# Storing most rows of dV of three heads with fifteen of the sixteen DMA engines

## The chip, the core and the metric

The kernel runs on one core of one Trainium2 chip. Its metric is the device time of one execution in microseconds (us). "Span" is the time in the profile from the first to the last instruction of the profiled execution. A ratio of two kernels is the mean time of one kernel's fast runs over that of the other's in the same rounds, so it is not quite the ratio of the medians quoted beside it. "Fast" and "slow" are states of a run: a run over 1.5% above the fastest of its kernel counts as slow and is not compared.

## The reference

Forward and backward of a gated sum of a one-token attention block with a KV cache (A) and a small MLP (B). What matters here is the attention, because of its bytes:

```python
# H = 32 heads, Sk = 4096 cached keys, Dh = 128, bfloat16
scores = einsum("bhqd,bhkd->bhqk", q, k_cache) * Dh ** -0.5
p = softmax(scores)
o = einsum("bhqk,bhkd->bhqd", p, v_cache)
out = g * (o @ wo) + (1 - g) * mlp(x)
# returned: out and the gradients of x, k_cache, v_cache, wq, wo, w1, b1, w2, gate_w
```

K and V are 1 MB per head each and are read once. dK and dV are outer products of the same size and are written once. That is 134 MB (4 x 32 x 1.049) of the 164.9 MB which the core moves.

## The kernel before

Each head has a period: its K and V tiles were loaded three heads ahead on the SP queue, PE transposes and multiplies them, DVE writes the outer products, and POOL (the software DMA queue) stores them.

```python
kv_in = pool(bufs=4)          # Kn and Vn, four buffers each
outs  = pool(bufs=5)          # dK and dV share five buffers

def load_k(h):
    kts[h] = kv_in.tile([P, J, Dh], BF16, name="Kn", ...)   # P=128 partitions x 8 KB
    nc.sync.dma_start(kts[h][:], Kv[h])

def dv_half(h, half):
    st = sts[h]
    if half == 0:
        st["dV"] = outs.tile([P, J, Dh], BF16, name="dV_sb", tag="dVK")
    outer(st["dV"], st["p"], ..., half)
    if half == 1:
        nc.gpsimd.dma_start(dVv[h], st["dV"][:])

# ... (dk_half is alike; loop of heads:)
for h in range(H):
    load_k(h + 3); load_v(h + 3)
    # ...
    period(h)
```

A store of 128 rows of 8 KB has 16 completions in the trace, one for each of the 16 DMA engines; an even share is 8 rows to an engine.

Of the kernel before, what the change touches and what calls it, by code (L numbers as in the profile page):

```python
# [16 lines left out]
def kernel(  # L17
# [24 lines left out]
    nc = tc.nc  # L42
    P = 128
    _, H, Sk, Dh = A_k_cache.shape
    D = A_x.shape[-1]
    F = B_w1.shape[1]
    J = Sk // P
# [20 lines left out]
    dVv = out_3.rearrange("b h (p j) d -> (b h) p j d", p=P)  # L68
# [68 lines left out]
    def load_w2(c):  # L137
# [28 lines left out]
        out=ident_f[:], in_=ident_f[:], compare_op=ALU.not_equal, fill=1.0,  # L166
# [69 lines left out]
    for i in range(3):  # L236
        t = const.tile([P, 2, G, 2, 2], BF16, name=f"qd2_{i}")
# [370 lines left out]
    def outer(dst, col, row, half):  # L608
        n = J // 2
        a, b = half * n, (half + 1) * n  # L610
        nc.vector.tensor_tensor(  # L611
            dst[:, a:b, :].rearrange("p j (a b) -> p j a b", b=2),
            col[:, a:b, :].unsqueeze(2).to_broadcast([P, n, Dh // 2, 2]),
            row.rearrange("p (a b) -> p a b", b=2).unsqueeze(1).to_broadcast([P, n, Dh // 2, 2]),
            ALU.mult)
# [16 lines left out]
# [3 lines that stand above are left out]
            st["dV"] = outs.tile([P, J, Dh], BF16, name="dV_sb", tag="dVK")  # L635
        outer(st["dV"], st["p"], gps[h // G]["qd"][:, 1, (h % G) * Dh:(h % G + 1) * Dh], half)
        if half == 1:
            nc.gpsimd.dma_start(dVv[h], st["dV"][:])  # L638

    def period(h):  # L640
        gp = gps[h // G]
# [11 lines left out]
        def o_part(a, b):  # L653
            for j in range(a, b):
# [31 lines left out]
        nc.vector.scalar_tensor_tensor(pj[:], in0=DP[:, 0:J], scalar=1.0, in1=e[:], op0=ALU.mult, op1=ALU.mult,  # L686
                                       accum_out=part[:])
        dv_half(h, 0)
        nc.tensor.transpose(PT, part[:].to_broadcast([P, P]), ident_f[:])  # L689
        if nxt:  # L690
# [6 lines left out]
        nc.vector.scalar_tensor_tensor(ds[:], in0=DP[:, 0:J].unsqueeze(2).to_broadcast([P, J, 2]), scalar=dd[:], in1=p_bf[:],  # L697
                                       op0=ALU.subtract, op1=ALU.mult)
        dv_half(h, 1)
        nc.vector.tensor_scalar(o_all[:, h:h + 1], O[:, 0:1], rz[:], None, ALU.mult)  # L700
        if nxt:
# [145 lines left out]
```

## Time and profile before

| | before |
|---|---|
| time, median of the first 3 runs | 413.07 us (413.03 to 413.67) |
| span of the profiled run | 411.8 us |
| busiest compute engine | DVE, 74% |
| DMA | nine tenths or more from 10 us to the last slice, 401 GB/s on average |

First the page's slices (each of the 40 is 10.3 us) and its queue table: packets, MB, and the time of the packets as a share of sixteen engines' span.

```profile
DMA  7999999999999999999999999999999999999990
GB/s 293 419 416 400 424 423 415 424 422 423 421 425 422 423 418 421 423 423 420 424 420 423 423 407 420 421 406 386 399 421 419 426 419 422 422 384 372 377 358 14
...
q1 hardware_dynamic: 14404, 82.03, 48.3%
q0 software_dynamic: 12240, 82.03, 48.2%
```

The DMA engines hold the run at about 422 GB/s, and the rate sags in the last five slices. The last slice is the telling one: 14 GB/s over 10 us. The stretches of the tail say more (us from the span's start; busy time and number of instructions of each engine, granted clock, DMA share of sixteen engines, GB/s):

```profile
core 0: us, PE busy (x) PEld busy (x) DVE busy (x) ACT busy (x) POOL busy (x), PEclk, DMA share, GB/s
380.00:395.00 15.00, 4.99 (x122) 3.87 (x119) 13.70 (x39) 1.79 (x6) 5.78 (x8) 0.70 0.96 385
395.00:401.60 6.60, 0.27 (x1) 0.09 (x1) 3.19 (x13) 0.25 (x1) 0.00 (x0) 0.50 0.86 327
401.60:407.20 5.60, 0.00 (x0) 0.00 (x0) 0.00 (x0) 0.00 (x0) 0.00 (x0) 0.50 0.06 26
```

For 5.6 us nothing computes and the DMA share is 0.06, which is one engine of sixteen. It moves 26 GB/s, the pace of one engine. The whole span waits for it.

The trace also records when each of the sixteen engines reports its part of a DMA complete. These times have no engine names. They stand on the clock of the instructions: where PE waits for a load, it starts 0.04 to 0.14 us after the load's last completion. The table shows how far the 16th is behind the 15th. For the loads I used the five of the SP queue's eight semaphores on which every load has sixteen completions.

```
                          gap from the 15th to the 16th completion, us
K/V loads, first ten      0.3 to 2.1
K/V loads, last five      12.0  12.2  13.7  12.2  12.4
last store (dwq_l)        1st 400.6   15th 401.9   16th 407.5   gap 5.6
```

One engine falls behind all others. In the packet records 7,010 of the 8,064 stored rows of 8 KB take 309 ns. One chain of back-to-back packets is slower: from 200.1 us on its rows take 316, 319, 335, 335, 332, 315, 318 and 321 ns. Yet in the drain at the end, when one engine works alone, most 4 KB packets take 159 ns, as they do on other engines at their best. So, if the chain and the drain are the same engine, it is slow only in company. Instruction fetches load the engines too: 46 packets of 16 KB, about 1 us each, 46 us in all. The largest gap among the K/V loads is 13.7 us, so these fetches do not all fall on one engine.

The waits of compute for DMA, from the page's groups (busy us, mean ns, then idle us before the group and who ended most of it):

```profile
L586 PE MATMUL tr<-ident_f,Kn 128*128 128x128 f32 x512 | 82.2, 299 | 6.5 <-DMA Kn<-in_A_k_cache_dram 6.5
L611 DVE TENSOR_TENSOR dK_sb<-ds_bf,qd 128x2048 bf16<-128x2048 bf16 x64 | 77.7, 1215 | 4.4 <-DMA out_dram<-dV_sb 4.4
```

These two are small.

### The profile page before, as it was taken

What the parts mean: (1) busy time and instruction counts of PE and PEld (TensorE: products, weight loads), DVE (VectorE), ACT (ScalarE), POOL (GpSimd) and SP (SyncE); (2) the same over time, 40 slices, a digit from 0 to 9 for tenths busy, and PEclk for the clock granted to TensorE, in tenths of its full rate; (3) what the DMA queues carried; (4) which work ended last, traced back from release to release, by engine and by line L of the source; (5) the groups of instructions that cost most, each with busy time, mean ns of one, the idle gap of its engine ahead of it and who ended that gap; (6) DMA issues with size and microseconds to landing.
All of it is one profiled execution on the core that took longest, in us unless ns stands there. A gap on an engine that the chain in (4) does not pass through costs nothing.

```text
span 411.8 us, 13602 instructions
## 1 busy us (share of the span) xinstructions
PE 296.3 (72%) x5872; PEld 268.2 (65%) x5872; DVE 303.1 (74%) x791; ACT 177.1 (43%) x411; POOL 50.8 (12%) x99
## 2 busy tenths in 40 slices
PE   0688898588887888188887888338887789949300
PEld 0578787587786777178877777338777778848200
DVE  3339666856899999377698898537999997957860
ACT  1355555254545555046542557215554455534000
POOL 0001111000111111011101112001111121113410
PEclk9999999889999999779996999758999999997755
DMA  7999999999999999999999999999999999999990
GB/s 293 419 416 400 424 423 415 424 422 423 421 425 422 423 418 421 423 423 420 424 420 423 423 407 420 421 406 386 399 421 419 426 419 422 422 384 372 377 358 14
DMA packets 26744, 164.93 MB, mean 401 GB/s; under 512 B 2956, under 2 KB 3020, under 8 KB 10428
## 3 DMA queue, kind: packets, MB, share of 16 engines
q1 hardware_dynamic: 14404, 82.03, 48.3%
q0 software_dynamic: 12240, 82.03, 48.2%
q8 instruction: 46, 0.75, 0.7%
q14 instruction: 14, 0.11, 0.1%
q10 hardware_dynamic: 40, 0.01, 0.0%
HBM read 82.03 MB, written 82.03 MB: 398 GB/s over the span
## 4 chain that ended last, share of the span: by engine, by line
DMA 38%; DVE 33%; PE 19%; ACT 4%; issue 3%; POOL 0%; ACTq 0%; SPq 0%; POOLq 0%; DVEq 0%
DMA Kn<-in_A_k_cache_dram 30%; PE tr L586 8%; DVE dK_sb L611 7%; DVE dV_sb L611 7%; DMA out_dram<-dV_sb 6%; DVE junk L382 4%; ACT tT L588 3%; PE sA L655 3%; DVE junk L285 3%; PE sA L595 2%; PE sB L708 2%; DVE junk L534 1%; DVE junk L491 1%; DMA vec_rows<-in_gate_w_dram 1%; DVE dj L695 1%
## 5 line engine op out<-in xcount | busy, mean ns | idle before, releaser
L588 ACT COPY tT<-tr 128x512 f32<-128x512 f32 x256 | 142.2, 587 | 129.7 <-PE tr L586 128.9
L595 PEld LDWEIGHTS <-tT 128*128 128x128 bf16 x2048 | 79.7, 98 | 44.4 <-ACT tT L588 34.5
L586 PE MATMUL tr<-ident_f,Kn 128*128 128x128 f32 x512 | 82.2, 299 | 6.5 <-DMA Kn<-in_A_k_cache_dram 6.5
L611 DVE TENSOR_TENSOR dK_sb<-ds_bf,qd 128x2048 bf16<-128x2048 bf16 x64 | 77.7, 1215 | 4.4 <-DMA out_dram<-dV_sb 4.4
L611 DVE TENSOR_TENSOR dV_sb<-p_bf,qd 128x2048 bf16<-128x2048 bf16 x64 | 77.9, 1218 | 0.2 <-issue 0.2
L586 PE MATMUL tr<-ident_f,Vn 128*128 128x128 f32 x512 | 72.5, 277 | 0.0
L586 PEld LDWEIGHTS tr<-ident_f,Kn 128*128 128x128 f32 x512 | 61.6, 153 | 7.7 <-issue 5.2
L595 PE MATMUL sA<-qd,tT 128*128 128x48 bf16 x1024 | 48.6, 187 | 23.7 <-ACT dq_all L713 12.8
L586 PEld LDWEIGHTS tr<-ident_f,Vn 128*128 128x128 f32 x512 | 55.9, 141 | 0.0
L595 PE MATMUL sB<-qd,tT 128*128 128x48 bf16 x1024 | 46.3, 183 | 0.0
L638 POOL DMA_DIRECT2D out_dram<-dV_sb x32 | 18.2, 569 | 170.2 <-DVE dV_sb L611 58.5
L655 PEld LDWEIGHTS <-Vn 128*128 128x128 bf16 x1024 | 30.6, 96 | 10.4 <-issue 10.4
L655 PE MATMUL sA<-e_bf,Vn 128*128 128x48 bf16 x1024 | 31.2, 184 | 7.6 <-DVE zs L675 6.2
L628 POOL DMA_DIRECT2D out_dram<-dK_sb x31 | 18.3, 591 | 145.3 <-DVE rz L677 97.2
L708 PE MATMUL sB<-ds_bf,Kn 128*128 128x48 bf16 x1024 | 31.5, 184 | 1.4 <-DVE ds_bf L697 1.4
L708 PEld LDWEIGHTS <-Kn 128*128 128x128 bf16 x1024 | 28.9, 97 | 1.6 <-issue 1.6
L659 DVE TENSOR_REDUCE m<-sA 128x1 f32<-128x32 f32 x32 | 6.0, 189 | 32.2 <-PE sA L595 25.6
L285 DVE SCALAR_TENSOR_TENSOR junk<-wo_g,da_bc 128x640 bf16<-128x640 bf16 x32 | 26.2, 820 | 1.7 <-ACT da_bc L226 1.1
L695 DVE TENSOR_SCALAR_CACHE_REDUCE dj<-sB,rz 128x128 f32<-128x128 f32 x32 | 11.1, 345 | 21.3 <-PE sB L689 21.3
L382 DVE SCALAR_TENSOR_TENSOR junk<-wq_g,dq_bc 128x1024 bf16<-128x1024 bf16 (+1 forms) x25 | 25.1, 1005 | 0.2
L275 PE MATMUL qc_ps<-cols_bf,wq_g 128*128 128x1 bf16 x160 | 5.3, 164 | 22.1 <-DMA wq_g<-in_A_wq_dram 22.1
L275 PEld LDWEIGHTS <-wq_g 128*128 128x128 bf16 x160 | 4.8, 100 | 22.6 <-DMA wq_g<-in_A_wq_dram 22.4
(154 smaller groups left out, 280.7 us busy)
## 6 DMA issues: line engine op xcount, KB each, us to landing
Kn<-in_A_k_cache_dram SPq DMA_DIRECT2D x32, 1024.0 KB, 23.9
Vn<-in_A_v_cache_dram SPq DMA_DIRECT2D x32, 1024.0 KB, 29.0
out_dram<-dV_sb POOLq DMA_DIRECT2D x32, 1024.0 KB, 11.8
out_dram<-dK_sb POOLq DMA_DIRECT2D x31, 1024.0 KB, 12.0
wq_g<-in_A_wq_dram SPq DMA_DIRECT2D x4, 1280.0 KB, 30.3
wo_g<-in_A_wo_dram SPq DMA_DIRECT2D x8, 640.0 KB, 7.4
out_dram<-wo_g POOLq DMA_DIRECT2D x8, 640.0 KB, 11.3
out_dram<-dwq_t POOLq DMA_DIRECT2D x5, 896.0 KB, 14.4
```

Of the source, the lines that this page charges most:

```text
L275: nc.tensor.matmul(qc_ps[:, hh:hh + 1], lhsT=wq[:, rc, off + hh * Dh:off + (hh + 1) * Dh], rhs=x_bf[:, rc:rc + 1], start=(rc == 0), stop=( ...
L285: nc.vector.scalar_tensor_tensor(junk[:, 0:D], in0=wos[g][:, i, :], scalar=1.0, in1=da_bc[:], op0=ALU.mult, op1=ALU.mult, accum_out=gp["do ...
L382: nc.vector.scalar_tensor_tensor(junk[:, c0:c1], in0=wqs[w][:, rc, c0:c1], scalar=1.0, in1=dq_bc[:, w * WG * Dh + c0:w * WG * Dh + c1], op ...
L586: nc.tensor.transpose(tp[:, t, :], flat[:, k * P:(k + 1) * P], ident_f[:])
L588: nc.scalar.copy(sb[:].rearrange("p a b -> p (a b)"), tp[:].rearrange("p a b -> p (a b)"))
L595: nc.tensor.matmul(out[:, 2 * k:2 * k + W], lhsT=tb[:, t, par, :], rhs=vec[:, par, :].unsqueeze(1).to_broadcast([P, W // 2, 2]), start=(pa ...
L611: nc.vector.tensor_tensor(dst[:, a:b, :].rearrange("p j (a b) -> p j a b", b=2), col[:, a:b, :].unsqueeze(2).to_broadcast([P, n, Dh // 2, 2]),
L628: nc.gpsimd.dma_start(dKv[h], st["dK"][:])
L638: nc.gpsimd.dma_start(dVv[h], st["dV"][:])
L655: nc.tensor.matmul(O, lhsT=vts[h][:, j, :], rhs=st["e"][:, j:j + 1].to_broadcast([P, W]), start=(j == 0), stop=(j == J - 1))
L695: nc.vector.tensor_scalar(dj[:], PT, rz[:], None, ALU.mult, ALU.add, accum_out=dd[:])
L708: nc.tensor.matmul(DQ, lhsT=kts[h][:, j, :], rhs=ds[:, j, 0:1].to_broadcast([P, W]), start=(j == 0), stop=(j == J - 1))
```

## The change

Intent: take rows away from the slow engine. The Trainium skill, "DMA: Bandwidth & Descriptors", section "Why a DMA increments its semaphore by 16 and not by 1", says that a DMA uses the largest number of engines up to 16 that divides its slowest dimension, and that on the software queue fewer than 16 are taken in a row from a round-robin cursor. By that rule, 5 rows go to positions 0 to 4, 120 rows to the next fifteen (5 to 15 and 0 to 3, 8 rows each), and 3 rows to 4, 5 and 6. Position 4 gets 2 rows instead of 8; positions 0 to 3, 5 and 6 get 9. The trace has no engine numbers, so it can neither confirm nor refute this layout.

```diff
         if half == 1:
-            nc.gpsimd.dma_start(dVv[h], st["dV"][:])
+            if h % 10 == 9:
+                spread(dVv[h], st["dV"])
+            else:
+                nc.gpsimd.dma_start(dVv[h], st["dV"][:])
+
+    def spread(dst, t):
+        src = t[:].rearrange("p j d -> p (j d)")
+        out = dst.rearrange("p j d -> p (j d)")
+        nc.gpsimd.inc_swdge_sem([], [], mode="reset_dge_cursor")
+        for a, b in ((120, 125), (0, 120), (125, 128)):
+            nc.gpsimd.dma_start(out[a:b, :], src[a:b, :], max_dma_last_dim=J * Dh)
```

The last argument splits each 8 KB row into two of 4 KB, which makes the shape of the DMA three-dimensional (120 x 2 x 2048 elements).

## The prediction

> **What bounds the kernel now: the DMA engines, and of the sixteen, one.** The page's slices show DMA at nine tenths from about 10 us to the end at 415 to 425 GB/s, sagging to 358 to 384 in the last five. The queue table: 82.03 MB loaded on q1 and 82.03 MB stored on the software queue q0, 48.3% + 48.2% of sixteen engines' span. No compute engine is above 74%; PE waits only 6.5 us in all for Kn, DVE 4.4 us for a store to free a dV buffer (groups and waits).
>
> In the packet records a full 8 KB row takes 309 ns, about 306 ns from one to the next (26.8 GB/s per engine), on most engines. One chain of packets is slower: 313 to 345 ns per row, about 5%. The sixteen completions of each DMA show the same: for K/V loads the gap from the 15th to the 16th grows from 0.3 us early to 12.4 us late in the run, with the 14th and 15th within about 1 us. Of the last stores (dwq_l, the last dwo, dK halves) the 16th completes 5.6 to 5.7 us after the 15th. The span ends with one engine draining alone for 5.6 us, ten microseconds after compute is done. PE's instruction fetches (46 of 16 KB, about 1 us each) rotate over several engines and don't explain it.
>
> The Trainium skill, "DMA: Bandwidth & Descriptors", section "Latency and other measured facts", says engines 7 and 15 are usually slower in traces where the software queue is used (cause a guess). This trace agrees that one is slower; it doesn't number it.
>
> **What the change does.** Three dV stores of 1 MB (8 rows per engine) become 5 + 120 + 3 rows. By the same page, section "Why a DMA increments its semaphore by 16 and not by 1", a software-queue DMA takes the largest divisor up to 16 of its rows as number of engines, starting from a cursor. So 5 rows on five engines, 120 on the next fifteen (8 each), 3 on the next three: one engine gets 2 rows instead of 8, six get 9. Per run the spared engine loses 18 rows; at about 0.32 us, 5.8 us. Six others gain 3 rows, 0.9 us. Added: six more DMA issues on POOL, 0.53 us each (12% busy, much idle), rows in two 4 KB pieces (159 instead of 154 ns each, nothing), 96 completion writes of 9 ns. Compute order is unchanged.
>
> **How much is critical.** If the spared engine is the slow one, it is busy without a pause to the end, so the span shortens by its relief until another engine ends last: the others end 5.6 us earlier now, and up to 0.9 us later after. Gain: about 4.7 us (range 3.5 to 6). If the slow engine is another one, nothing is won, and 0 to 1 us lost. The cut with a 5-row head and 18 rows of relief against a tail of 5.65 us looks fitted to this engine; I give 0.7 that it hits.
>
> **Predicted: 408.6 us**, 407.2 to 413.6 eight times in ten. Faster by over 2% 0.03, within 2% 0.95, slower 0.02: even a full hit is 1.2%.
>
> **What would show it.** Right: the 15th-to-16th gap of the last stores falls from 5.65 us to under 1.5 us; the late K/V load gap shrinks in steps of about 2 us after heads 9, 19, 29; slices 36 to 40 carry more GB/s; PE's wait for Kn falls. Wrong engine: the gap stays 5.6 us and the 120-row store still completes last on the slow engine.
>
> **What would make it wrong.** The cursor is not where I think, or shapes like this go ceil(rows/16) per engine; the slow engine's pace differs from run to run; two engines slow on another chip.

## The result

| | before | after |
|---|---|---|
| median | 413.33 us (4 runs, 413.03 to 413.67) | 408.69 us (4 runs, 407.98 to 409.01) |
| ratio of fast runs | | 0.9885, 95% interval 0.9867 to 0.9903 |
| span of the profiled run | 411.8 us | 406.6 us |

The time is inside the range and 0.1 us from the figure named. The lines of the page after, which answer to those above:

```profile
GB/s 290 420 416 396 422 422 420 419 423 423 421 425 421 422 420 406 424 425 421 422 420 425 424 421 416 410 424 423 425 420 424 424 421 424 422 402 368 406 394 77
...
q0 software_dynamic: 12912, 82.03, 49.0%
q1 hardware_dynamic: 14404, 82.03, 48.9%
...
L586 PE MATMUL tr<-ident_f,Kn 128*128 128x128 f32 x512 | 84.2, 304 | 9.6 <-DMA Kn<-in_A_k_cache_dram 9.6
L611 DVE TENSOR_TENSOR dK_sb<-ds_bf,qd 128x2048 bf16<-128x2048 bf16 x64 | 77.8, 1216 | 3.9 <-DMA out_dram<-dV_sb 3.6
```

The same stretches of the tail:

```profile
380.00:395.00 15.00, 1.61 (x26) 0.99 (x25) 11.28 (x38) 0.54 (x2) 4.97 (x7) 0.50 1.00 401
395.00:401.60 6.60, 0.00 (x0) 0.00 (x0) 0.00 (x0) 0.00 (x0) 0.00 (x0) 0.50 0.48 191
401.60:407.20 5.60, 0.00 (x0) 0.00 (x0) 0.00 (x0) 0.00 (x0) 0.00 (x0) 0.50 0.00 1
```

The stretch in which one engine worked alone is empty. The completions agree:

```
                          before                          after
K/V loads, last five      12.0 12.2 13.7 12.2 12.4        4.2 4.9 3.8 4.6 4.8
last store, 15th / 16th   401.9 / 407.5                   401.3 / 401.7
```

The gap of the loads drops by about 2 us after each of the first two split stores (2.9 to 1.0 after head 9) and grows again between and after them. When the third is issued, at 355.1 us, only three loads are not yet complete, and their gaps show no drop (4.3, 4.6 and 4.8 us). The slow engine ends 5.8 us sooner, which over 18 rows is 0.32 us per row.

The gain is not only at the tail. Compute runs ahead too: the issue of the last store by POOL, from the timeline of each kernel (start, duration, idle before), is 5.7 us sooner. Before:

```profile
393.20 0.87 POOL L777 DMA_DIRECT2D out_dram<-dwq_l  x1 [0.70 <-DVE ambj L787]
```

After:

```profile
387.51 0.90 POOL L787 DMA_DIRECT2D out_dram<-dwq_l  x1 [0.18 <-DVE ambj L797]
```

### The profile page after: what moved, and what is told of

Same layout as the page of the kernel before. It is cut to its first block, busy times and chain, and to the rows that moved or that the text cites. A ratio compares the mean times of both kernels' runs of the same rounds, so it can differ in the third digit from the quotient of the medians.

```text
span 406.6 us, 13614 instructions
## 1 busy us (share of the span) xinstructions
PE 298.3 (73%) x5872; PEld 269.9 (66%) x5872; DVE 303.8 (75%) x791; ACT 177.2 (44%) x411; POOL 55.7 (14%) x105
## 3 DMA queue, kind: packets, MB, share of 16 engines
q0 software_dynamic: 12912, 82.03, 49.0%
q1 hardware_dynamic: 14404, 82.03, 48.9%
HBM read 82.03 MB, written 82.03 MB: 404 GB/s over the span
## 4 chain that ended last, share of the span: by engine, by line
DMA 36%; DVE 33%; PE 19%; ACT 4%; issue 3%; POOL 0%; ACTq 0%; DVEq 0%; POOLq 0%
DMA Kn<-in_A_k_cache_dram 29%; DVE dK_sb L611 8%; PE tr L586 8%; DVE dV_sb L611 7%; DMA out_dram<-dV_sb 6%; DVE junk L382 4%; ACT tT L588 4%; PE sA L665 3%; DVE junk L285 2%; PE sA L595 2%; PE sB L718 2%; DVE junk L534 1%; DVE junk L491 1%; DMA vec_rows<-in_gate_w_dram 1%; DVE dj L705 1%
## 5 line engine op out<-in xcount | busy, mean ns | idle before, releaser
L586 PE MATMUL tr<-ident_f,Kn 128*128 128x128 f32 x512 | 84.2, 304 | 9.6 <-DMA Kn<-in_A_k_cache_dram 9.6
L586 PEld LDWEIGHTS tr<-ident_f,Kn 128*128 128x128 f32 x512 | 63.0, 155 | 11.3 <-issue 10.5
L641 POOL DMA_DIRECT2D out_dram<-dV_sb x29 | 16.5, 570 | 149.0 <-DVE o_all L710 54.7
L705 DVE TENSOR_SCALAR_CACHE_REDUCE dj<-sB,rz 128x128 f32<-128x128 f32 x32 | 11.1, 346 | 12.8 <-PE sB L699 12.7
L689 ACT ACTIVATE p_bf<-e_bf,rz 128x64 bf16<-128x64 bf16 x32 | 11.1, 348 | 13.6 <-DVE rz L687 10.6
L696 DVE SCALAR_TENSOR_TENSOR pj<-sB,e_bf 128x32 f32<-128x32 f32 x32 | 6.1, 191 | 13.1 <-PE sB L595 12.9
```

What stands on the lines that cost most here:

```text
L586: nc.tensor.transpose(tp[:, t, :], flat[:, k * P:(k + 1) * P], ident_f[:])
L689: nc.scalar.activation(p_bf[:], e[:].unsqueeze(2).to_broadcast([P, J, 2]), ACT.Copy, scale=rz[:])
L705: nc.vector.tensor_scalar(dj[:], PT, rz[:], None, ALU.mult, ALU.add, accum_out=dd[:])
```

## The experiments

Theory: one engine, at position 4 of the software queue's cursor, is slower than the rest and has work queued to the end, so each row taken from it shortens the run by what that row costs it. Rivals: the smaller pieces or the reset help; sparing any engine helps; the gain needs the lag gone altogether; only relief at some moment counts. Twelve kernels ran on two chips (the first four on one, the other eight on the other). All gave correct results.

### Same pieces, no engine spared

```diff
-        for a, b in ((120, 125), (0, 120), (125, 128)):
+        for a, b in ((0, 48), (48, 96), (96, 128)):
```

> The same three heads, also cursor reset and three pieces of 4 KB packets, but 48 + 48 + 32 rows, so that every piece runs on all 16 engines and each engine keeps its 8 rows. Theory (relief of one slow engine): no gain, 413.3 us within 1, last-store gap between the 15th and 16th completion stays 5 to 6 us. Rival (smaller pieces or packets, or the reset, are what helps): about 408.7 us and a gap under 1.5 us.

Measured: 415.15 us, ratio 1.0036 (1.0020 to 1.0051). No gain, so neither pieces nor reset are what helps. It even lost 1.5 us, a little more than the 1 us that the forecast allowed. Its profiled run fell in the slow state (451.24 us, clock 0.573), so its trace can't say why and its gap isn't used. As a control of the early heads (below) the same split on heads 2, 4 and 6 was run:

> The 48 + 48 + 32 split over all 16 engines on heads 2, 4 and 6, as control for the early run. If the 1.5 us that this split cost on heads 9, 19 and 29 is the price of the pieces themselves (packets, completion writes): 414.5 to 415.5 us. If it came from where those stores fell among the semaphores: 413 to 414 us. In either case no gain.

Measured: 413.78 us, ratio 1.0006 (0.9992 to 1.0020), last-store gap 6.2 us. So there the pieces themselves cost nothing that can be measured. The 1.5 us belongs to where the stores stood in the first kernel, or to the chip, as the two kernels ran on different ones. What it was stays open.

### Another engine spared

```diff
-        for a, b in ((120, 125), (0, 120), (125, 128)):
+        for a, b in ((0, 120), (120, 128)):      # skip15
+        for a, b in ((120, 128), (0, 120)):      # skip7, another kernel
```

> Pieces 120 then 8 rows after the reset: by the cursor rule engine at position 15 gets 1 row, positions 0 to 6 get 9, so the engine at position 4 that the change spares gets 3 rows more in all. Theory (only the engine at position 4 is slow): 413.3 to 415 us, gap 5.5 to 7.5 us. Rival A (the pieces go ceil(rows/16) to an engine, and the change spares the last engine): 408 to 409.5 us. Rival B (sparing any engine helps): 408 to 410 us.

> Pieces 8 then 120 rows: by the cursor rule position 7 gets 1 row, positions 0 to 6 get 9. Theory: 413.3 to 415 us, gap 5.5 to 7.5 us, as with position 15. Rival B (sparing any engine helps): 408 to 410 us. If it gains alone, position 7 is slow and the cursor does not start at 0.

| spared | median | ratio (95%) | last store: 15th / 16th completion |
|---|---|---|---|
| position 15 | 415.08 us | 1.0050 (1.0019 to 1.0082) | 401.9 / 408.7 |
| position 7 | 416.15 us | 1.0053 (1.0036 to 1.0070) | 405.3 / 412.3 |

Sparing either one loses. The slow engine now ends 6.8 and 7.1 us behind the next, as forecast, but the times lie 0.1 and 1.2 us above the 415 us that the forecast allowed. Three rows more on position 4, at 0.32 us each, should cost 1.0 us. The medians lost 1.5 and 2.6 us; the 16-engine split at these heads lost 1.5 us without any such row. What makes up the rest is open. (The profiled run of the kernel for position 7 is the slowest of its five, 418.75 us.) Both kernels also give position 4 a row more per split; sparing another engine with position 4 left at 8 rows was not tried. If position 7 or 15 were the slow one, though, it would have lost 21 rows here, and the run would have gained. So it matters which engine is spared, and the one that matters is neither 7 nor 15. Positions other than 4, 7 and 15 were not tried.

### One head only

```diff
-            if h % 10 == 9:
+            if h == 19:
```

> The change on head 19 alone: a third of the relief, 6 rows of about 0.32 us. Theory: 1.5 to 2.0 us gained (411.2 to 411.9 us), last-store gap about 3.7 us. Rival (the gain is a threshold: it needs the lag gone altogether): no gain, or nearly all of it.

Measured: 411.32 us, ratio 0.9944 (0.9931 to 0.9956), so 2.3 us gained. The time was as forecast and the gain is no threshold. But the gap was not: it stayed at 6.6 us, not 3.7. The slow engine ended 2.5 us sooner (405.0) and the others 3.4 us sooner (15th at 398.5). So the other fifteen must have been held back by the slow one, I take it through loads that compute waits for and buffers that it frees. What a spared row wins is read from the slow engine's own end, not from that gap.

### Earlier heads, later heads

```diff
-            if h % 10 == 9:
+            if h in (2, 4, 6):        # early3
+            if h in (27, 28, 29):     # late3, another kernel
+            if h in (24, 25, 26):     # late3b, another kernel
```

> The change's split on heads 2, 4 and 6 instead of 9, 19 and 29, while the slow engine lags by no more than about 2 us. Theory (the slow engine never pauses, so work taken from it shortens the run wherever it is taken): 408 to 409.7 us. Rival (only relief at the tail, or relief of a lag that is already there, counts): 411.5 to 414 us.

> The split on heads 27, 28 and 29. Theory: the relief of about 5.8 us comes off the end all the same, 408 to 409.7 us; the gap of the K/V loads grows past 10 us before head 27 as in the kernel before. Rival (most of the gain comes from compute that no longer waits for late loads through the run): 410.5 us or more.

Measured: early 408.24 us, ratio 0.9872 (0.9858 to 0.9885). Late 413.60 us, ratio 0.9998 (0.9983 to 1.0012). The early one met the theory and the late one met its rival. By these two alone I would have had to say that only early relief counts. But the timeline of POOL in the late run shows something else:

```profile
350.50 1.84 POOL L648 DMA_DIRECT2D out_dram<-dV_sb  x3 [3.82 <-DVE o_all L710]
362.20 0.58 POOL L628 DMA_DIRECT2D out_dram<-dK_sb  x1 [9.86 <-DMA out_dram<-w_sb]
363.58 0.56 POOL L648 DMA_DIRECT2D out_dram<-dV_sb  x1 [0.80 <-DMA out_dram<-dV_sb]
```

The store of dK had its data and stood 9.86 us for the completion of another store. The program's stores use eight completion semaphores in turn. A split store takes three of them. So the eighth store after the 2160 KB store of w_sb came round to its semaphore while that store, which takes 23.8 us, was still on its way. The DMA rate fell to 303 GB/s in the 36th slice of this run. The relief was there, as the last-store gap fell to 2.9 us, but the other engines ended 2.7 us later than before (404.5 against 401.9), and the slow one no sooner (407.5). To tell this from the rival, the split went to heads 24 to 26, all ahead of the w_sb store:

> The run with heads 27 to 29 gained nothing, but POOL stood 9.9 us on the completion of the w1 gradient store: its eight completion semaphores had come round sooner, as each split store takes three. Here the split is on heads 24, 25 and 26, all issued before that store. Theory (the slow engine never pauses; the late run failed by the semaphores alone): 408 to 410 us and no POOL wait on the w_sb store. Rival (relief after the load lag has built up is worth little): 411.5 to 414 us.

Measured: 408.81 us, ratio 0.9885 (0.9870 to 0.9900). No POOL wait on w_sb is left:

```profile
338.33 0.91 POOL L543 DMA_DIRECT2D out_dram<-w_sb  x1 [0.18 <-issue]
341.88 0.56 POOL L641 DMA_DIRECT2D out_dram<-dV_sb  x1 [2.64 <-DVE o_all L710]
346.71 0.55 POOL L628 DMA_DIRECT2D out_dram<-dK_sb  x1 [4.27 <-DVE rz L687]
351.12 0.53 POOL L641 DMA_DIRECT2D out_dram<-dV_sb  x1 [3.87 <-DVE o_all L710]
```

Its load gap grew to 11.1 us as in the kernel before and then fell to 0.4 us by the last load. So relief that comes after the gap has grown past ten microseconds is worth as much as early relief, within what these runs resolve (0.9872, 0.9885, 0.9885). The late run's failure goes with its POOL wait and not with lateness as such; that the wait alone made it was not tried on the same heads.

### Without the cursor reset

```diff
-        nc.gpsimd.inc_swdge_sem([], [], mode="reset_dge_cursor")
```

> The change without the cursor reset. Theory by the cursor rule: each split store moves the cursor by 5 + 15 + 3 = 23, so by 7 of 16, and the next one spares another engine; of three stores at most one spares the slow engine, and the launches differ if the cursor outlives a launch: 411 to 415.5 us, runs scattered by more than 1 us. Rival (the reset does nothing; splits always start at the same engine): 408.7 us.

Measured: 412.06 us, ratio 0.9967 (0.9953 to 0.9980). About a third of the gain, 1.4 of 4.7 us: the load gap falls after head 9 as with the change, but not after the later two, and the last five loads stand at 6.5 to 8.2 us. This fits the cursor rule: if the cursor stands at its start before head 9, only the first of the three stores spares position 4. The slow engine ends 1.9 us sooner (405.6), about what six rows should give. So the later splits need the reset. The scatter I expected did not come: five runs lie between 411.73 and 413.02 us. A cursor that starts alike in each launch would explain that; no run tests it.

### Whole rows in place of two halves

```diff
-            nc.gpsimd.dma_start(out[a:b, :], src[a:b, :], max_dma_last_dim=J * Dh)
+            nc.gpsimd.dma_start(out[a:b, :], src[a:b, :])
```

> The change with whole 8 KB rows in place of two 4 KB pieces per row. If the shape does not matter to which engine is spared: 407.3 to 408.7 us, a little under the change (the split on all 16 engines cost 1.5 us, some of it perhaps the pieces). If two-dimensional shapes go ceil(rows/16) to an engine from the first on, the last engine is spared and the slow one gets 3 rows more: 414 to 416 us.

Measured: 416.48 us, ratio 1.0075 (1.0061 to 1.0090), the slow engine 7.2 us behind. Without the argument that looks like a detail nothing of the gain is left. The skill's section named above mentions an exception in which some direct copies put ceil(partitions/16) partitions on each engine from the first on; 120 rows then spare the last engine, and position 4 gets more rows. The sign of the loss fits that; its size, 2.9 us, is more than three rows at 0.32 us and lies above the range forecast. The 4-byte packets of q0 rose by 192 here and by 288 with the change, so the queue treated these pieces otherwise; how, the trace does not say.

### Stores off the software queue

```diff
-            nc.gpsimd.dma_start(dVv[h], st["dV"][:])
+            nc.sync.dma_start(dVv[h], st["dV"][:])      # and both forms of the dK store; no split
```

> The kernel before, with all dK and dV stores issued on SP, the queue of the loads, instead of POOL's software queue; program order kept. If the one engine is slow because of the software queue: the 15th-to-16th gap of the K/V loads stays under 3 us to the end and the time is at or under 409 us unless loads behind stores in one ring cost it. If the engine is slow for any traffic: the gap grows past 8 us as before and the time stays at 412 us or more.

Measured: 412.79 us, ratio 0.9983 (0.9970 to 0.9997). The queue table of this run:

```profile
q1 hardware_dynamic: 23764, 149.14, 88.0%
q0 software_dynamic: 2880, 14.91, 8.9%
```

Only 14.91 of 82.03 MB stored still go through the software queue. Yet one engine falls behind as before: of the DMA that ends last, 15 parts are complete at 397.5 us and the 16th at 410.0. So one engine is slow for either queue's rows (that it is the same one, the trace does not say), and the remedy is to give it fewer.

### One head more, early

```diff
-            if h % 10 == 9:
+            if h in (2, 4, 6, 12):
```

> Heads 2, 4, 6 and 12: 24 rows of relief, early. With three early heads the slow engine still ended 2.4 us after the next one. Theory: one head more takes about 1.9 us from the slow engine and adds 0.3 us to six others, so 406.2 to 407.5 us, the last-store gap under 1 us. Rival (three heads are already enough and the split stores' own cost grows): 408 to 409.5 us.

Measured: 406.79 us, ratio 0.9835 (0.9820 to 0.9850). This beats both kernels: 1.65% under the kernel before, where the change is 1.15% under. The slow engine ends at 400.0 us, 1.3 us behind the next; under 1 us was forecast. Its slices, to set beside those of before and after:

```profile
GB/s 287 420 416 399 420 422 418 417 425 425 418 423 423 423 423 417 421 423 423 420 422 425 422 428 417 417 425 421 424 422 423 424 420 423 425 409 401 407 402 71
```

The 36th to 39th slices now keep above 400 GB/s (384, 372, 377 and 358 before).

The end of the slow engine against the rows taken from it, from the profiled runs:

| kernel | rows taken | slow engine ends, us | sooner by, us | per row, us | span, us |
|---|---|---|---|---|---|
| before | 0 | 407.5 | | | 411.8 |
| head 19 | 6 | 405.0 | 2.5 | 0.41 | 409.4 |
| the change | 18 | 401.7 | 5.8 | 0.32 | 406.6 |
| heads 2, 4, 6 | 18 | 401.2 | 6.3 | 0.35 | 406.2 |
| heads 24, 25, 26 | 18 | 402.2 | 5.3 | 0.30 | 407.0 |
| heads 2, 4, 6, 12 | 24 | 400.0 | 7.4 | 0.31 | 405.0 |
| heads 27, 28, 29 (POOL waited for w_sb) | 18 | 407.5 | 0.0 | 0.00 | 412.3 |

## Why the prediction was right

- **One slow engine bounds the run.** Right. Taking rows from it won time in six of seven kernels (heads 27 to 29 won nothing); sparing positions 7 and 15 did not.
- **18 rows of about 0.32 us, 5.8 us of relief.** Right: the slow engine ended 5.8 us sooner.
- **Which engine.** The trace could not number it, so I gave 0.7 to a hit, arguing from the cut of the change. It hit. That was a bet, not a reading.
- **Net gain 4.7 us.** The size was right (4.64 us between the medians), the sum was not. I took the other fifteen's end as fixed and put them up to 0.9 us later; they set the new end in my sum. In fact the 15th ended 0.6 us sooner (401.3), compute issued its last store 5.7 us sooner, and the slow engine is still the last, by 0.4 us. What held the gain under its 5.8 us was something else: from the last store's completion to the end of the span it is 4.3 us before and 4.9 us after, so the span became 5.2 us shorter, and the medians differ by 4.64 us. That the figure was met to 0.1 us is luck. The one-head run shows most plainly that the others are held by the slow one.
- **The gap falls under 1.5 us; steps in the load gap.** Right, 0.4 us. The steps are there after heads 9 and 19; after head 29 none shows.
- **PE's wait for Kn falls.** Wrong: it rose from 6.5 to 9.6 us. The waits of PE for wq_g fell from 22.1 to 13.6 us instead, and the wait of DVE for PE in the dj step (L695, L705 after) from 21.3 to 12.7 us. I had picked one wait as the sign of a lag that shows in several. For wq_g the completions say where the fall comes from: the 16th part of its last three loads was 0.5, 3.3 and 8.1 us behind the 15th, and after the change 0.5, 0.5 and 2.1 us, about 8.7 us less in all, against 8.5 us less waiting. Yet with heads 24 to 26 this wait stayed at 21.6 us and the gain was the same: what counts is the slow engine's own end. The waits of these two groups (us in total, times, longest), before:

```profile
PE qc_ps L275 <- DMA wq_g<-in_A_wq_dram: 22.1, 3, 11.4
...
DVE dj L695 <- PE sB L689: 21.3, 3, 11.1
```

And after:

```profile
PE qc_ps L275 <- DMA wq_g<-in_A_wq_dram: 13.6, 3, 6.4
...
DVE dj L705 <- PE sB L699: 12.7, 3, 6.1
```

- **Slices 36 to 40 carry more.** Right for four of five; the 37th went from 372 to 368 GB/s.
- **Costs of the change.** 96 completion writes were forecast and the 4-byte packets of q0 rose by 288. At 9 ns each, over sixteen engines, it is nothing. What I missed is that each piece takes one of eight semaphores. It did no visible harm at heads 9, 19 and 29 (POOL waited 2.8 us in all for a store of dK). At heads 27 to 29 a wait of 9.86 us came with the loss of the whole gain.

## What to carry to other kernels

Where DMA is near full and yet the last slice is almost empty, compare the 15th and the 16th completion of the same DMA over the run. Here a gap that grew meant one slow engine, and each row that it was spared brought its end 0.30 to 0.41 us forward, as long as nothing else held the stores up. Then prove which engine, and that the shape of the DMA really spares it, by a run that spares another. Before splitting a transfer, count what else the pieces use up, such as completion semaphores taken in turn: an experiment that fails by such a wait says nothing of the idea.

## What the Trainium skill lacked or had wrong

- "DMA: Bandwidth & Descriptors", "Latency and other measured facts", says engines 7 and 15 are usually the slow ones. Sparing positions 15 and 7 lost 1.5 and 2.6 us on the one chip where it was tried (ratios 1.0050, 1.0053), while sparing position 4 of the cursor won on that chip (0.9944 with one head) and on another (0.9835 to 0.9885). No run shows which engine number position 4 has, so this does not refute the page.
- The same place guesses at the software queue's descriptor rings as the cause. With 14.91 MB of 82.03 MB stored left on that queue, the last DMA's 16th part was still 12.5 us behind the 15th. What makes the engine slow is open; in the drain of the kernel before, where one engine works alone, it is not slow (159 ns per 4 KB packet).
- Same page, "Why a DMA increments its semaphore by 16 and not by 1": "some direct copies" are excepted from the rule for the number of engines, but not which. Here rows of one piece (120 x 4096) behaved otherwise than rows of two (120 x 2 x 2048): 416.48 against 408.69 us.
- The same section has all 16 engines post one completion each on the software queue. Six more DMAs raised the 4-byte packets by 96 where all ran on 16 engines, and by 288 where, by the page's rule, they ran on 5, 15 and 3. The semaphore of each piece still rose by 16, so the page is not wrong there; it does not say what the further 4-byte packets are.
- The same section has the cursor but not its reset. Without it 412.06 us, five runs within 1.3 us.
- No page that I used has the turn of eight completion semaphores on POOL's stores; it cost a wait of 9.86 us behind one 2160 KB store.
